# Retention of the first four chunks in whole chunks of 128 tokens, and the first pieces of the first product cut in 256 and 128 tokens

## The chip, the cores and the metric

The kernel runs on one core of a Trainium2 chip. The metric is the time of one execution on the device in microseconds; the kernel before takes 969.51 us (median of three runs, 968.78 to 971.09). The engines are named as in the profile: PE is TensorE (matrix products), PEld its loading of weights, DVE VectorE, ACT ScalarE, POOL GpSimd, SP the engine that issues most transfers.

## The reference

Retention (an attention with decay instead of a softmax) over 8 batches, 8 heads, 576 tokens and 64 columns per head, and then a feed-forward layer with a squared ReLU. All is float32.

```python
def _attn_ref(q, k, v):                      # (8, 8, 576, 64) each
    scale = 1.0 / np.sqrt(D_)
    scores = scale * np.matmul(q, k.transpose(0, 1, 3, 2))
    gamma = 1.0 - 2.0 ** (-5.0 - np.arange(H, dtype=np.float32))
    rel = pos[:, None] - pos[None, :]
    Dmat = np.where(rel >= 0, gamma[:, None, None] ** rel[None, :, :], 0.0)
    ret = scores * Dmat[None, :, :, :]
    return np.matmul(ret, v)

def _moe_ref(x, w_in, w_out):                # (4608, 512), (512, 2048), (2048, 512)
    h = np.maximum(x @ w_in, 0.0)
    return h * h @ w_out

# x: the retention's output as (batch * tokens, heads * columns)
```

## The kernel before

Each batch is cut in chunks of 128 tokens (the last has 64). A chunk is *turned* (q and k are transposed on TensorE, and the result is copied from PSUM by ScalarE and VectorE), its *scores* are computed and masked, and its output x is the sum of what its own tokens give (`own`) and what the state of all earlier tokens gives (`carry`, with the state copied to `u_sb`); the state itself grows in PSUM (`grow`). The decay stands in factors by which q and v are multiplied, so the mask holds only ones and zeros.

The kernel before works within a chunk by halves of 64 tokens. Every product then has 64 rows and 64 columns, and there is one state copy (`grown`) for each half:

```python
    def score(i, hp):
        for h in range(chunks[i][3] // CH):                     # CH = 64: two halves
            for e in range(2):
                t = slice(CH * h, CH * h + CH)
                nc.tensor.matmul(st[i]["sc"][e][rows(h), hp, :], lhsT=st[i]["kT"][rows(e), hp, t], rhs=st[i]["qT"][rows(e), hp, t],
                                 start=True, stop=True, skip_group_check=True)

    def retain_a(i):
        ...
        beside_each(own_of(i, 1, 1), grow_of(i, 0), range(0, H, 2))   # own of half 1 beside grow of half 0
        grown(i, 0)                                                    # state copy on ScalarE

    def retain_b(i):
        ...
        for h in reversed(range(cs // CH)):
            if 2 * ci + h == 0:
                continue
            u = u_sb[(2 * ci + h) % 3]
            for hp, e, b in HEADS[0:2] + HEADS[4:6] + HEADS[2:4] + HEADS[6:8]:
                s["read"] = nc.tensor.matmul(
                    x_at(hp, e, b, h), lhsT=u[rows(e), hp, :], rhs=s["qT"][rows(e), hp, CH * h:CH * h + CH], ...)

    def retain_c(i):
        ...
        own, grow = own_of(i, 0, 0), grow_of(i, 1) if more else []
        beside_each(own, grow, (0, 2))
        wait_for(st[i]["read"])
        beside_each(own, grow, (4, 6))
        x_out(i, lambda: grown(i, 1) if more else None)                # x to SBUF, then the state copy
```

The feed-forward layer works on blocks of 512 tokens. Its weights come in 64 bits and are converted on the chip, piece by piece (16 pieces of 128 columns for the first product). A piece takes six steps: three passes of VectorE and two of ScalarE, two shorter passes of VectorE ahead of them for the bits; `convert(n)` issues the next n. The first block, block 0, is multiplied piece by piece (`first_in`) while the weights are still being converted, so that TensorE has work between the chunks. A piece can run on the first 256 tokens (`halves=(0,)`) as soon as chunks 0 and 1 have given their x:

```python
    def first_in(j, halves=(0, 1)):
        ...
        for c in range(N_DM):                                          # 4
            nc.tensor.matmul(p.rearrange("p h t -> p (h t)"), lhsT=w[:, c, :], rhs=xT[0][:, c, lo * HT:hi * HT],
                             start=(c == 0), stop=(c == N_DM - 1))
        ...
        nc.scalar.activation(t, p, AF.Relu)
```

The profile shows each of these float32 products as two instructions (two MATMUL and two LDWEIGHTS).

The opening, in program order (loads and scalings left out):

```python
    scores(0); turn(1); retain_a(0); convert(3); scores(1)
    retain_b(0); retain_c(0); convert(2)
    retain_a(1); convert(4); retain_b(1); retain_c(1); convert(3)
    first_in(0, (0,)); turn(2); convert(3); first_in(1, (0,)); scores(2)
    retain_a(2); convert(2); retain_b(2); retain_c(2); convert(1)
    turn(3); convert(3); first_in(2, (0,)); scores(3); convert(3)
    retain_a(3); turn(4); convert(2); retain_b(3); retain_c(3)
    step(); step(); scores(4); convert(6); step(); convert(3); step(); convert(3)
    for i in range(N_EARLY + 1, N_CH + 1):      # the loop over the other chunks
        ...
```

`step()` runs the next part of the feed-forward layer: here the second halves of pieces 0, 1 and 2 and then piece 3 in full.

Of the kernel before, what the change touches and what calls it, by code (L numbers as in the profile page):

```python
# [9 lines left out]
F32 = mybir.dt.float32  # L10
# [30 lines left out]
def kernel(  # L41
# [91 lines left out]
    def load(i, names="qkv"):  # L133
        b, ci, c0, cs = chunks[i]
        if i == 0:
            nc.sync.dma_start(dv, decays)
        got = loaded.setdefault(i, [None] * 3)
        for name, pool, src in (("q", ld3, q), ("k", ld5, k), ("v", ld4, v)):
            if name not in names:
                continue  # L140
            t = got["qkv".index(name)] = pool.tile([128, H, D], F32, tag=name, name=f"{name}_ld")

            issue = nc.scalar if i == 0 and name != "q" else nc.sync
            at = src[b, :, c0:c0 + cs, :].rearrange("h s d -> s h d")
            if name == "v":
                issue.dma_start(t[:cs], at)
            else:

                for e in range(2):
                    issue.dma_start(t[:cs, e * HP:(e + 1) * HP, :], at[:, e::2, :])  # L150
# [6 lines left out]
    pieces += [(1, mq + mh * N_MQ, e) for mq in range(N_MQ) for mh in range(2) for e in range(2)]  # L157
    N_W1 = N_DF
    N_ALONE = 3
    N_HALF = 3  # L160
    stage = [W[5].rearrange("p (o s f) -> p o s f", o=4, s=NP),
             W[6][:, 0:3 * NP * 128].rearrange("p (o s f) -> p o s f", o=3, s=NP)]
    N_RAW = 8
# [10 lines left out]
    def rows(half, n=64):  # L174
        return slice(64 * half, 64 * half + n)
# [145 lines left out]
    def convert(count):  # L321
        for _ in range(count):
            f = next(w_in_steps, None)
            f and f()
# [18 lines left out]
    for half in range(2):  # L343
        at = slice(CH * half, CH * half + CH)
        nc.gpsimd.affine_select(
            out=msk[at, 0, 0, :], in_=msk[at, 0, 0, :], compare_op=ALU.is_ge, fill=0.0, base=0,
            pattern=[[1, CH]], channel_multiplier=-1,
        )
    u_sb = [only.tile([128, HP, D], F32, name=f"u_sb{j}") for j in range(3)]


# [9 lines left out]
    def head(hp, e):  # L361
        return 4 * (hp % 2) + 2 * e + hp // 2
# [6 lines left out]
    def clears(half, bank):  # L369

        new = (half, bank) not in clean
        clean.add((half, bank))
        return new

    def scale_q(i, engine):
        ci, cs = chunks[i][1], chunks[i][3]
        t = loaded[i][0][:cs]
        engine.tensor_tensor(t, t, dv[:cs, :, NCH + ci:NCH + ci + 1].to_broadcast([cs, H, D]), op=ALU.mult)  # L378
# [69 lines left out]
    def turn(i, engines=(0, 1)):  # L448
        turn_in(i)
        turn_out(i, engines)  # L450

    def scores(i, part=False):

        b_, ci, c0, cs = chunks[i]
        if i < N_EARLY:

            sc = [ps_f.tile([128, 512], F32, tag="f", name="sc_ps")[:, 0:256].rearrange("p (h t) -> p h t", h=HP) for e in range(2)]
        else:
            both = ps_t[0].tile([128, 2, 512], F32, tag="t", name="sc_ps")[:, :, 0:256].rearrange("p e (h t) -> p e h t", h=HP)
            sc = [both[:, e, :, :] for e in range(2)]  # L460
        st[i]["sc"] = sc
        st[i]["both"] = None if i < N_EARLY else both
        if part:
            return
        for hp in range(HP):
            score(i, hp)
        masked(i)
# [33 lines left out]
    def retain_a(i):  # L501

        b_, ci, c0, cs = chunks[i]
        xp[0] = ps_x.tile([128, 2, 256], F32, tag="x", name="x_ps", padded_shape=[128, 2, 512])
        clean.clear()
        if cs < C:
            return
        beside_each(own_of(i, 1, 1), grow_of(i, 0), range(0, H, 2))
        grown(i, 0)

    def retain_b(i):

        s = st[i]
        b_, ci, c0, cs = chunks[i]
# [6 lines that stand above are left out]
                    x_at(hp, e, b, h), lhsT=u[rows(e), hp, :], rhs=s["qT"][rows(e), hp, CH * h:CH * h + CH],  # L521
                    start=clears(b, e), stop=False, skip_group_check=True)

    def retain_c(i):

        b_, ci, c0, cs = chunks[i]
        more = ci + 1 < NCH
# [3 lines that stand above are left out]
        beside_each(own, grow, (4, 6))  # L531
        x_out(i, lambda: grown(i, 1) if more else None)

    def x_out(i, after):

        b_, ci, c0, cs = chunks[i]
        tok = b_ * S + c0
        at = tok
        p = xp[0][:, :, 0:256].rearrange("p a (g t) -> p a g t", g=2)
        while at < tok + cs:  # L540
            n = at // TOK

            while steps and steps[0][0] <= n - 2:
                if i >= N_ONE:
                    move(2)
                step()
            end = min(tok + cs, (n + 1) * TOK)
            nc.scalar.copy(xT[n][:, :, at - n * TOK:end - n * TOK].rearrange("p (g a) t -> p a g t", a=2),  # L548
                           p[:, :, :, at - tok:end - tok])
            if at == tok:  # L550
                after()
            at = end
            if n_next[0] < N_BLK and (n_next[0] + 1) * TOK <= at:
                steps.extend(block_steps(n_next[0]))
                n_next[0] += 1
        st[i] = loaded[i] = None
# [106 lines left out]
            f and f()  # L663
        del queue[:count]

    def first_in(j, halves=(0, 1)):

        assert n_made[0] > j
        wi, m, e = pieces[j]
        mp, mm = divmod(m, 2)  # L670
        p = ps_f.tile([128, 2, HT], F32, tag="f", name="h_ps")
        w = w_in[mp][:, mm, 2 * e:2 * e + 2, :, :].rearrange("p s c f -> p (s c) f")
        lo, hi = halves[0], halves[-1] + 1
        p = p[:, lo:hi, :]
        for c in range(N_DM):
            nc.tensor.matmul(p.rearrange("p h t -> p (h t)"), lhsT=w[:, c, :], rhs=xT[0][:, c, lo * HT:hi * HT],  # L676
                             start=(c == 0), stop=(c == N_DM - 1))

        t = g_room[mp % 2][:, 2:5:2, mm, :] if e else g_room[mp % 2][:, 0:4:3, mm, :]
        t = t[:, lo:hi, :]  # L680
        nc.scalar.activation(t, p, AF.Relu)

        some(2)
        queue.append(lambda: nc.vector.tensor_tensor(t, t, t, op=ALU.mult))
        if mm and e and hi == 2:
            queue.append(lambda: [nc.sync.dma_start(
                g_dram[0, a:b, :, 2 * mp:2 * mp + 2, :].rearrange("s p m t -> p s (m t)"),
                g_room[mp % 2][:, a:b, :, :].rearrange("p s m t -> p s (m t)")) for a, b in QUARTERS])
        if j >= N_W1 - 4:

            sums_w.setdefault(0, sum_w_in(0)).pop(0)()
            if n_next[0] > 1:
                if 1 not in sums_x:
                    sums_x[1] = sum_x(1)
                sums_x[1].pop(0)()
# [75 lines left out]

    def block_steps(n):
        if n == 0:
            seconds = [(0, first_in, j, (1,)) for j in range(N_HALF)]
            return seconds + [(0, first_in, j) for j in range(N_HALF, N_W1)]
        return [(n, ffn_in, n, mp, j) for mp in range(N_MP) for j in range(NP)]

    def step():
        n, f, *args = steps.pop(0)
        done[0] += 1  # L780
        f(*args)
# [77 lines left out]
    load(3)  # L859
    fetch_raw(2)  # L860
    warm(1)
    scores(0)
    turn(1)
    retain_a(0)
    convert(3)
    scores(1)
    scale_q(2, nc.gpsimd)
    retain_b(0)
    retain_c(0)
    load(4)  # L870
    fetch_raw(3)
    convert(2)
    retain_a(1)
    convert(4)
    retain_b(1)
    retain_c(1)
    load(5)
    convert(3)
    first_in(0, (0,))
    turn(2)  # L880
    convert(3)
    first_in(1, (0,))
    scores(2)
    scale_q(3, nc.gpsimd)
    retain_a(2)
    convert(2)
    retain_b(2)
    retain_c(2)
    load(6)
    convert(1)  # L890
    turn(3)
    convert(3)
    first_in(2, (0,))
    scores(3)
    scale_q(4, nc.gpsimd)
    convert(3)
    retain_a(3)
    early.close()
    ps_t[0] = first.enter_context(tc.tile_pool(name="ps_t", bufs=1, space=PS))
    turn(4)  # L900
    convert(2)
    retain_b(3)
    retain_c(3)
    load(7)
    step()
    step()
    scores(4)
    convert(6)
    scale_q(5, nc.gpsimd)
    step()  # L910
    convert(3)
    step()
    convert(3)
    for i in range(N_EARLY + 1, N_CH + 1):
# [290 lines left out]
```

## Time and profile before

| | kernel before |
|---|---|
| time, median of three runs | 969.51 us |
| span of the profiled execution | 966.2 us |
| TensorE busy | 948.0 us, 98% |
| VectorE busy | 783.2 us, 81% |
| ScalarE busy | 338.0 us, 35% |
| mean granted TensorE clock | 0.994 |

The page has the busy time of each engine, then the span in 40 equal slices of some 24 us, in which a digit is the busy share in tenths; the row PEclk is the clock that TensorE was granted, in tenths of its full speed. The other views used are the busy time by stage, and an engine's instructions in order of time. In the latter a line has the start and the length in us, the engine and the line of the code, the operation with what it writes and reads, how many there are, and in brackets how long the engine was idle before and what ended that. "issue" there means that nothing the profile shows was waited for. L432 is the turn, L473 the scores, L565 grow, L571 own, L520 carry, L676 a piece of block 0's first product, L499 the state copy, L548 the copy of x, L483 the mask and L213 to L231 the conversion of weights.

### The profile page before, as it was taken

What the parts mean: (1) busy time and instruction counts of PE and PEld (TensorE: products, weight loads), DVE (VectorE), ACT (ScalarE), POOL (GpSimd) and SP (SyncE); (2) the same over time, 40 slices, a digit from 0 to 9 for tenths busy, and PEclk for the clock granted to TensorE, in tenths of its full rate; (3) what the DMA queues carried; (4) which work ended last, traced back from release to release, by engine and by line L of the source; (5) the groups of instructions that cost most, each with busy time, mean ns of one, the idle gap of its engine ahead of it and who ended that gap; (6) DMA issues with size and microseconds to landing.
All of it is one profiled execution on the core that took longest, in us unless ns stands there. A gap on an engine that the chain in (4) does not pass through costs nothing. (4 is left out here: it accounts for less than half of the span.)

```text
span 966.2 us, 23674 instructions
## 1 busy us (share of the span) xinstructions
PE 948.0 (98%) x10002; PEld 851.0 (88%) x10002; DVE 783.2 (81%) x1447; ACT 338.0 (35%) x808; POOL 134.4 (14%) x121
## 2 busy tenths in 40 slices
PE   7899999999999999999999999999999999999998
PEld 5655688888888888878888899999999999999998
DVE  4689799988799897977966597888888787887876
ACT  3445475866765766657621000000000000000000
POOL 3301233214123123122110000000000000000000
PEclk8999999999999999999999999999999999999999
DMA  9974668677757857765178966445354454524251
GB/s 225 241 220 115 164 179 207 182 237 202 204 149 226 240 154 203 217 196 165 58 259 334 357 243 256 154 154 185 128 190 163 160 193 169 199 99 174 89 175 44
DMA packets 170730, 181.40 MB, mean 188 GB/s; under 512 B 116864, under 2 KB 131200, under 8 KB 163968
## 3 DMA queue, kind: packets, MB, share of 16 engines
q1 hardware_dynamic: 168528, 179.37, 59.7%
q8 instruction: 78, 1.28, 0.6%
q10 hardware_dynamic: 2096, 0.52, 0.2%
q14 instruction: 28, 0.23, 0.1%
HBM read 109.36 MB, written 70.52 MB: 186 GB/s over the span
## 5 line engine op out<-in xcount | busy, mean ns | idle before, releaser
L712 PE MATMUL h_b<-room,w 128*128 128x256 f32 x768 | 183.6, 382 | 2.1 <-DVE room L731 1.8
L415 ACT COPY qk<-flip 32x256 f32<-32x256 f32 x416 | 167.4, 402 | 6.1
L712 PEld LDWEIGHTS h_b<-room,w 128*128 128x128 f32 x768 | 144.1, 190 | 24.0 <-DVE room L731 3.3
L1054 PE MATMUL o_b<-w,room 128*128 128x128 f32 x1168 | 144.4, 275 | 0.2 <-DVE room L1006 0.2
L1054 PEld LDWEIGHTS o_b<-w,room 128*128 128x128 f32 x1168 | 137.3, 192 | 0.4 <-DVE room L1006 0.4
L712 PE MATMUL h_a<-room,w 128*128 128x256 f32 x512 | 122.4, 381 | 2.0 <-issue 2.0
L1054 PE MATMUL o_c<-w,room 128*128 128x128 f32 x1008 | 123.0, 275 | 0.0
L712 PE MATMUL h_c<-room,w 128*128 128x256 f32 x512 | 121.7, 380 | 0.0
L1054 PEld LDWEIGHTS o_c<-w,room 128*128 128x128 f32 x1008 | 117.7, 192 | 0.0
L712 PEld LDWEIGHTS h_a<-room,w 128*128 128x128 f32 x512 | 96.3, 190 | 15.8 <-issue 2.4
L1068 ACT COPY r<-o_a 128x128 f32<-128x128 f32 x53 | 14.1, 266 | 271.6 <-PE o_a L1054 230.9
L712 PEld LDWEIGHTS h_c<-room,w 128*128 128x128 f32 x512 | 96.7, 190 | 13.3
L1054 PE MATMUL o_a<-w,a 128*128 128x128 f32 x688 | 85.6, 275 | 0.0
L729 POOL TENSOR_TENSOR room<-room 128x512 f32<-128x512 f32 x32 | 35.9, 1121 | 336.4 <-ACT room L728 336.4
L1054 PEld LDWEIGHTS o_a<-w,a 128*128 128x128 f32 x688 | 81.2, 192 | 0.1
L719 DVE SCALAR_TENSOR_TENSOR room<-room 128x512 f32<-128x512 f32 x96 | 70.4, 733 | 3.3
L676 PE MATMUL h_ps<-room,w 128*128 128x512 f32 (+1 forms) x152 | 61.1, 551 | 2.5 <-ACT room L548 1.3
L571 PEld LDWEIGHTS x_ps<-qk,v_ld 64*64 64x64 f32 x1152 | 44.3, 135 | 19.4 <-issue 16.1
L571 PE MATMUL x_ps<-qk,v_ld 64*64 64x64 f32 x1152 | 55.4, 224 | 5.8 <-issue 2.5
L378 POOL TENSOR_TENSOR q_ld<-q_ld,dv 128x512 f32<-128x512 f32 (+1 forms) x39 | 46.4, 1189 | 87.0 <-DMA q_ld<-in_q_dram 80.7
L492 POOL TENSOR_TENSOR v_ld<-v_ld,dv 128x512 f32<-128x512 f32 (+1 forms) x40 | 53.2, 1332 | 6.6 <-DMA v_ld<-in_v_dram 6.6
L676 PEld LDWEIGHTS h_ps<-room,w 128*128 128x128 f32 x152 | 29.1, 199 | 24.4 <-issue 19.6
(105 smaller groups left out, 1348.5 us busy)
## 6 DMA issues: line engine op xcount, KB each, us to landing
g_dram<-room SPq DMA_DIRECT2D x32, 1280.0 KB, 5.7
a<-g_dram SPq DMA_DIRECT2D x30, 1024.0 KB, 6.0
room<-g_dram SPq DMA_DIRECT2D x15, 1024.0 KB, 6.1
w<-w_dram SPq DMA_DIRECT2D x7, 1792.0 KB, 11.0
out_dram<-room SPq DMA_DIRECT2D x17, 512.0 KB, 3.2
q_ld<-in_q_dram SPq DMA_DIRECT2D x64, 128.0 KB, 5.2
w<-in_moe_w_in_dram SPq DMA_DIRECT2D x16, 512.0 KB, 6.3
w<-in_moe_w_out_dram SPq DMA_DIRECT2D x16, 512.0 KB, 4.2
```

The costliest lines, as they stand in the source:

```text
L378: engine.tensor_tensor(t, t, dv[:cs, :, NCH + ci:NCH + ci + 1].to_broadcast([cs, H, D]), op=ALU.mult)
L415: nc.scalar.copy(*moves.pop(0)[2:])
L492: nc.gpsimd.tensor_tensor(vs[:cs], vs[:cs], dv[:cs, :, ci:ci + 1].to_broadcast([cs, H, D]), op=ALU.mult)
L571: return [lambda hp=hp, e=e, b=b: nc.tensor.matmul(x_at(hp, e, b, h), lhsT=s["vs"][rows(h), head(hp, e), :], rhs=s["ret"][rows(h), e, hp, ...
L676: nc.tensor.matmul(p.rearrange("p h t -> p (h t)"), lhsT=w[:, c, :], rhs=xT[0][:, c, lo * HT:hi * HT], start=(c == 0), stop=(c == N_DM - 1))
L712: nc.tensor.matmul(p[:, mm, :], lhsT=w[:, c, :], rhs=xs[n][right][:, c, :], start=(j in OPENS and mm == 0 and c == 0), stop=(j in CLOSES a ...
L719: nc.vector.scalar_tensor_tensor(t, t, 0.0, t, op0=ALU.max, op1=ALU.mult)
L729: nc.gpsimd.tensor_tensor(g["A11"], g["A11"], g["A11"], op=ALU.mult)
L1054: nc.tensor.matmul(p, lhsT=s["lefts"][left][:, m, :], rhs=w_out[j][:, m, WO_SLOT[right], :], start=(i in OPENS and m == 0), stop=(i in CLO ...
L1068: nc.scalar.copy(r[:, 0, 0:128], p)
```

## The change

In the first four chunks the products take the whole chunk of 128 tokens. The scores are 128 x 128 under a full triangular mask, own and grow contract over 128 tokens, and the state is copied once for a chunk. What this is for is half as many products and instructions and one state copy less in the chain of every chunk. The other chunks stay as they are. Of block 0, two pieces instead of three are begun early. Their first 256 tokens run after chunk 1, the tokens of chunk 2 (128) while chunk 3 is masked, and the last 128 after chunk 3. The order of turns, conversions and steps in the opening is arranged anew.

```diff
-    N_HALF = 3
+    N_HALF = 2
+    ret_room = [room[:, 7168 + j * 1024:8192 + j * 1024].rearrange("p (e a t) -> p e a t", e=2, a=HP) for j in range(2)]
+    msk_full = room[:, 9216:9344].rearrange("p (a t) -> p a t", a=1)
+    nc.gpsimd.memset(msk_full, 1.0)
+    nc.gpsimd.affine_select(... pattern=[[1, C]], channel_multiplier=-1)
...
+    def scores_full(i):
+        sc = st[i]["sc"] = [ps_f.tile([128, HP, C], F32, tag="f", name="sc_ps") for e in range(2)]
+        for hp in range(HP):
+            for e in range(2):
+                nc.tensor.matmul(sc[e][:, hp, :], lhsT=st[i]["kT"][rows(e), hp, :], rhs=st[i]["qT"][rows(e), hp, :],
+                                 start=True, stop=True, skip_group_check=True)
+        r = st[i]["ret"] = ret_room[i % 2]
+        for e in range(2):
+            nc.vector.tensor_tensor(r[:, e, :, :], sc[e], msk_full.to_broadcast([C, HP, C]), op=ALU.mult)
+        scale_v(i)
+    def carry_full(i):
+        ...
+        if chunks[i][1] == 0:
+            u_ps[0] = ps_u.tile([128, HP, D], F32, tag="u", name="u_ps")
+            return
+        u = u_sb[2 * chunks[i][1] % 3]
+        for hp, e, b in HEADS[0:2] + HEADS[4:6] + HEADS[2:4] + HEADS[6:8]:
+            nc.tensor.matmul(x_full(hp, e, b), lhsT=u[rows(e), hp, :], rhs=st[i]["qT"][rows(e), hp, :], ...)
+    def retain_full(i):
+        ci = chunks[i][1]
+        for hp, e, b in (HEADS[j] for j in (0, 4, 2, 6, 1, 5, 3, 7)):
+            nc.tensor.matmul(x_full(hp, e, b), lhsT=st[i]["vs"][:, head(hp, e), :], rhs=st[i]["ret"][:, e, hp, :], ...)
+        for hp, e, b in HEADS:
+            nc.tensor.matmul(u_ps[0][rows(e), hp, :], lhsT=loaded[i][1][:, 2 * hp + e, :], rhs=st[i]["vs"][:, head(hp, e), :], ...)
+        x_out(i, lambda: grown(i, 1))
...
-    def first_in(j, halves=(0, 1)):
+    def first_in(j, halves=(0, 1), at=(0, HT)):
...
-            seconds = [(0, first_in, j, (1,)) for j in range(N_HALF)]
+            seconds = [(0, first_in, j, (1,), (C, HT)) for j in range(N_HALF)]
...
-    scores(0)
-    turn(1)
-    retain_a(0)
+    scores_full(0)
+    turn(1, (0, 0))
+    carry_full(0)
+    retain_full(0)
     convert(3)
-    scores(1)
+    scores_full(1)
     scale_q(2, nc.gpsimd)
-    retain_b(0)
-    retain_c(0)
+    carry_full(1)
+    convert(3)
+    retain_full(1)
     load(4)
     fetch_raw(3)
-    convert(2)
-    retain_a(1)
-    convert(4)
-    retain_b(1)
-    retain_c(1)
     load(5)
     convert(3)
     first_in(0, (0,))
-    turn(2)
     convert(3)
+    turn(2, (0, 0))
+    scores_full(2)
+    scale_q(3, nc.gpsimd)
+    carry_full(2)
     first_in(1, (0,))
-    scores(2)
-    scale_q(3, nc.gpsimd)
-    retain_a(2)
-    convert(2)
-    retain_b(2)
-    retain_c(2)
+    convert(3)
+    retain_full(2)
     load(6)
-    convert(1)
     turn(3)
-    convert(3)
-    first_in(2, (0,))
-    scores(3)
+    scores_full(3)
     scale_q(4, nc.gpsimd)
     convert(3)
-    retain_a(3)
+    carry_full(3)
+    for j in range(N_HALF):
+        first_in(j, (1,), (0, C))
     early.close()
     ps_t[0] = first.enter_context(tc.tile_pool(name="ps_t", bufs=1, space=PS))
-    turn(4)
-    convert(2)
-    retain_b(3)
-    retain_c(3)
+    retain_full(3)
     load(7)
+    convert(5)
     step()
     step()
+    turn(4)
+    convert(3)
+    step()
     scores(4)
+    scale_q(5, nc.gpsimd)
     convert(6)
-    scale_q(5, nc.gpsimd)
-    step()
-    convert(3)
     step()
     convert(3)
```

In `turn(i, (0, 0))` both copies of the turned q and k are ScalarE's; otherwise ScalarE and VectorE have one each.

More of the change, by code (lines that the diff above doesn't have):

```diff
@@ L348 @@
         )
+    ret_room = [room[:, 7168 + j * 1024:8192 + j * 1024].rearrange("p (e a t) -> p e a t", e=2, a=HP) for j in range(2)]
+    msk_full = room[:, 9216:9344].rearrange("p (a t) -> p a t", a=1)
+    nc.gpsimd.memset(msk_full, 1.0)
+    nc.gpsimd.affine_select(
+        out=msk_full[:, 0, :], in_=msk_full[:, 0, :], compare_op=ALU.is_ge, fill=0.0, base=0,
+        pattern=[[1, C]], channel_multiplier=-1,
+    )
     u_sb = [only.tile([128, HP, D], F32, name=f"u_sb{j}") for j in range(3)]
@@ L532, in retain_c, with x_full @@
         x_out(i, lambda: grown(i, 1) if more else None)
+    def scores_full(i):
[8 more added lines that the diff above has]
+        scale_v(i)
+    def x_full(hp, e, b):
+        return xp[0][rows(b), e, 0:256].rearrange("p (g t) -> p g t", g=2)[:, hp % 2, :]
+    def carry_full(i):
+        xp[0] = ps_x.tile([128, 2, 256], F32, tag="x", name="x_ps", padded_shape=[128, 2, 512])
+        clean.clear()
+        if chunks[i][1] == 0:
[3 more added lines that the diff above has]
+        for hp, e, b in HEADS[0:2] + HEADS[4:6] + HEADS[2:4] + HEADS[6:8]:
+            nc.tensor.matmul(x_full(hp, e, b), lhsT=u[rows(e), hp, :], rhs=st[i]["qT"][rows(e), hp, :],
+                             start=clears(b, e), stop=False, skip_group_check=True)
+    def retain_full(i):
+        ci = chunks[i][1]
+        for hp, e, b in (HEADS[j] for j in (0, 4, 2, 6, 1, 5, 3, 7)):
+            nc.tensor.matmul(x_full(hp, e, b), lhsT=st[i]["vs"][:, head(hp, e), :], rhs=st[i]["ret"][:, e, hp, :],
+                             start=clears(b, e), stop=False, skip_group_check=True)
+        for hp, e, b in HEADS:
+            nc.tensor.matmul(u_ps[0][rows(e), hp, :], lhsT=loaded[i][1][:, 2 * hp + e, :], rhs=st[i]["vs"][:, head(hp, e), :],
+                             start=(ci == 0 and hp == 0), stop=(hp == HP - 1), skip_group_check=True)
+        x_out(i, lambda: grown(i, 1))
     def x_out(i, after):
@@ L673, in first_in @@
         lo, hi = halves[0], halves[-1] + 1
-        p = p[:, lo:hi, :]
+        p = p[:, lo:hi, at[0]:at[1]]
         for c in range(N_DM):
-            nc.tensor.matmul(p.rearrange("p h t -> p (h t)"), lhsT=w[:, c, :], rhs=xT[0][:, c, lo * HT:hi * HT],
+            nc.tensor.matmul(p, lhsT=w[:, c, :], rhs=xT[0][:, c, :].rearrange("p (h t) -> p h t", h=2)[:, lo:hi, at[0]:at[1]],
                              start=(c == 0), stop=(c == N_DM - 1))
         t = g_room[mp % 2][:, 2:5:2, mm, :] if e else g_room[mp % 2][:, 0:4:3, mm, :]
-        t = t[:, lo:hi, :]
+        t = t[:, lo:hi, at[0]:at[1]]
         nc.scalar.activation(t, p, AF.Relu)
@@ L684, in first_in @@
         queue.append(lambda: nc.vector.tensor_tensor(t, t, t, op=ALU.mult))
-        if mm and e and hi == 2:
+        if mm and e and hi == 2 and at[1] == HT:
             queue.append(lambda: [nc.sync.dma_start(
```

## The prediction

> **What bounds the kernel now.** I read the page's busy shares and slices first, then a table of busy time by stage over the first 60 us, then TensorE's own order of time, then the waits. The page:
>
> ```profile
> span 966.2 us, 23674 instructions
> ...
> PE 948.0 (98%) x10002; PEld 851.0 (88%) x10002; DVE 783.2 (81%) x1447; ACT 338.0 (35%) x808; POOL 134.4 (14%) x121
> ...
> PE   7899999999999999999999999999999999999998
> ...
> PEclk8999999999999999999999999999999999999999
> ...
> PE 40%; DVE 1%; issue 0%; DVEq 0%
> ```
>
> TensorE is busy 98% of the span, so 18.2 us in all are idle, and the chain that ended last is TensorE's. Only the first two slices (24 us each) show gaps and a lower clock, and those are where the change works. By stage (columns: window, its length, busy us and count of PE, PEld, DVE, ACT, POOL, then the granted clock, DMA share, GB/s):
>
> ```profile
> 8.00:14.50 6.50, 5.17 (x192) 4.17 (x189) 5.11 (x11) 3.59 (x7) 3.13 (x3) 1.00 1.23 279
> 14.50:20.50 6.00, 2.48 (x72) 2.10 (x69) 3.79 (x5) 2.02 (x4) 2.24 (x2) 0.63 0.97 224
> 20.50:24.40 3.90, 3.73 (x10) 2.52 (x10) 0.85 (x2) 0.39 (x2) 2.53 (x2) 0.50 0.98 254
> 24.40:32.00 7.60, 6.05 (x155) 5.06 (x156) 4.98 (x9) 2.97 (x7) 2.32 (x2) 0.87 1.17 264
> 32.00:42.00 10.00, 7.05 (x164) 5.70 (x165) 6.91 (x14) 4.51 (x10) 4.17 (x4) 1.00 0.98 212
> 42.00:50.00 8.00, 8.00 (x45) 5.67 (x44) 5.18 (x12) 3.50 (x7) 2.20 (x3) 1.00 0.96 278
> ```
>
> From 8 to 42 us TensorE idles 1.33 + 3.52 + 0.17 + 1.55 + 2.95 = 9.5 us; from 42 to 100 us it does not idle at all (58.0 busy of 58.0). A further window, 16.1 to 26.3, has clock 0.50 and 8.1 us of TensorE work: about 4 us of that are lost to the clock. So **the most that an earlier start can give is 9.5 + 4 = 13.5 us, 1.4%**. TensorE's order of time names the gaps:
>
> ```profile
> 17.05 0.26 PE L571 MATMUL x_ps<-qk,v_ld 64*64 64x64 f32 x1 [2.54 <-issue]
> ...
> 18.01 1.13 PE L520 MATMUL x_ps<-qk,u_sb 64*64 64x64 f32 x32 [0.47 <-ACT u_sb L499]
> ...
> 20.66 3.78 PE L676 MATMUL h_ps<-room,w 128*128 128x256 f32 x8 [0.67 <-ACT room L548]
> ...
> 29.48 0.27 PE L571 MATMUL x_ps<-qk,v_ld 64*64 64x64 f32 x2 [1.01 <-DVE qk L483]
> ...
> 30.71 0.69 PE L520 MATMUL x_ps<-qk,u_sb 64*64 64x64 f32 x32 [0.54 <-ACT u_sb L499]
> ...
> 35.62 0.38 PE L676 MATMUL h_ps<-room,w 128*128 128x256 f32 x1 [0.95 <-issue]
> ...
> 41.13 3.72 PE L676 MATMUL h_ps<-room,w 128*128 128x256 f32 x16 [0.59 <-ACT room L548]
> ```
>
> The largest gap, 2.54 us, waits for no engine ("issue"). Counting matmuls from the start, it falls after the 221st (442 instructions with their weight loads); the one of 0.95 us falls about 250 matmuls, so some 500 instructions, later. The DMA view by half microsecond shows one packet of the instruction queue at 14.0 to 14.5, the next at 18.5 to 19.0. I take both gaps for the arrival of instructions, with the DMA engines full (share 1.2 to 1.4 from 12 to 16). The others are the chain of one chunk: mask (1.0), state copy (0.5), x copied out (0.6).
>
> [...] Here TensorE stopped at 14.5 and the clock was 0.50 from about 16.1[...]. [...]
>
> **The change, part by part.** (1) *Work of one chunk.* Before: 32 instructions each for scores, carry and two halves of own and grow at about 15 ns, 4 x 0.5 = 2.0 us. After: 16 of each of four. A 128-column instruction alone takes 124 ns (144.4 us over 1168, group L1054, o_b), so with two tiles 62, with four 31; grow streams 64 columns with two tiles, 37. Scores 16 x 62 = 1.0, carry 16 x 31 = 0.5, own 1.0, grow 0.6: 3.1 us. **TensorE gets no less work, but about 1 us more per chunk**, half of it beside the mask it would wait for. (2) *Instructions.* 64 matmuls instead of 128 in a chunk, each with a weight load: 500 fewer in all. A block of 256 took 3.6 us before the 2.54 us gap. It will now take some 9, where fetching needed about 6 (11 to 17.05), so both issue gaps, 3.5 us, go. (3) *Waits.* One state copy per chunk instead of two, and it lies behind the next chunk's scores: the 0.5 us gaps go. (4) *Masks.* 512 columns from PSUM instead of 256: 2 x 0.6 instead of 2 x 0.34 us on VectorE, +0.5 per chunk, partly on the path; both turn copies of chunks 1 and 2 on ScalarE, one after the other, +0.5 each. (5) *Pieces.* Two are split 256 + 128 + 128 instead of three by 256 + 256: 8 x 124 ns = 1.0 per quarter, 8 x 239 = 1.9 per half, equal within 0.1 us. The quarters fill the mask wait of chunk 3.
>
> The new order in time, from the same durations: scores 0 at 8.8, turn 1 until 10.4, mask 0 until 11.25, retain 0 until 12.35; scores 1 until 13.35, mask 1 until 14.75, retain 1 until 15.85 (before 20.0). Piece 0 is converted behind mask 1, so at 17.3, and its half runs until 19.2; turn 2, two copies and scores 2 until 22.1, carry, half of piece 1 until 24.5, retain 2 until 26.1; turn 3 and copies 27.7, scores 3 until 28.7, carry and two quarters until 31.2, retain 3 until 32.8, x out at 33.5. Data is there: in GpSimd's order of time the scaling of v, which waits for the load, begins at 11.8 for chunk 1, 18.3 for chunk 2 and 23.0 for chunk 3. Before, this point is 41.13: **7.6 us earlier**. At that point 2 quarters, piece 2 in full and turn 4 are owed (2.0 + 3.63 + 0.65 = 6.3) against 3 halves (5.7): minus 0.6. The conversion of weights is half a piece behind by program order (35 conversion steps written ahead of the loop against 38, six to a piece); VectorE has 9.6 us free from 42 to 100, but a stall or two, about 0.5 us, may show. Net **about 7 us: 969.5 - 7 = 962.5**.
>
> **The rivals.** *The clock falls anyway.* From 15.85 to 17.3 TensorE waits for piece 0 and works thinly around it. If the clock halves for 10 us again, 3 to 4 us of the gain go: about 966. I give it three in ten. *128x64 does not run in pairs.* Then own and grow cost 16 x (124 + 70) = 3.1 instead of 1.6: 1.5 more per chunk, 6 in all, about 968. For it speaks that no such shape is in the trace; against it, own and grow with 64 rows already put two column halves side by side at 15 ns. *Weights become the bound.* VectorE is 85 to 90% busy from 60 to 100; if pieces come late, TensorE gets gaps there and the gain melts, 965 to 969. Against it: it idled 35% until 42 and is fed in the same order. *All goes better*: shapes pair at 55 ns and the chain closes up, 9 us, 960.
>
> **Range and chances.** The ceiling of 13.5 us is 1.4%, so faster by over 2% is next to excluded; slower by over 2%, 19 us, would need a new wait in the dense part. 962.5, range 958 to 967.
>
> **What would show it.** Right: no issue gap over 0.5 us before 42; clock 1.00 from 14 to 30; scores at about 62 ns per instruction; the first 16 matmuls of the second halves near 33.5; TensorE without gaps from then on. Wrong: clock 0.50 after 16 us; own at 124 ns apart; gaps in front of the pieces (L676) waiting for VectorE or ScalarE between 35 and 100; x of chunk 3 later than 36.

## The result, and the profile after

The changed kernel takes **964.78 us** (four runs, 964.09 to 964.94) against 969.14 us of the kernel before in the same comparison: ratio 0.9954, 95% interval 0.9932 to 0.9976. It is faster by 4.4 us; 7 were predicted. The changed kernel scatters by 0.9 us. The kernel before scatters far more: its runs in all comparisons lie mostly between 964 and 971 us, and its median in a comparison between 967.1 and 969.1 us. Against the largest of these comparisons (28 runs, 967.47 us) the changed kernel would be only 2.7 us faster.

The same rows of the page as before the change:

```profile
span 963.2 us, 23158 instructions
...
PE 947.4 (98%) x9754; PEld 849.4 (88%) x9754; DVE 784.6 (81%) x1446; ACT 337.4 (35%) x807; POOL 134.5 (14%) x123
...
PEclk9999999999999999999999999999999999999999
```

In the changed kernel L439 is the turn, L450 its copy, L547 the scores, L551 the mask, L573 own, L576 grow, L722 a piece of block 0's first product, L594 the copy of x and L758 the first product of block 1. TensorE has 248 products fewer, no slice with a lower clock any more, and, over the whole span, the same busy time. By stage (columns as in the prediction):

```profile
8.00:14.50 6.50, 5.81 (x103) 4.92 (x106) 3.77 (x6) 3.43 (x7) 3.38 (x3) 1.00 1.22 277
14.50:20.50 6.00, 4.41 (x68) 3.51 (x60) 5.66 (x9) 2.91 (x6) 2.12 (x2) 1.00 1.01 224
20.50:24.40 3.90, 2.74 (x42) 2.23 (x38) 2.55 (x5) 1.07 (x2) 2.47 (x2) 1.00 0.96 258
24.40:32.00 7.60, 6.70 (x102) 5.82 (x100) 3.89 (x7) 3.06 (x7) 2.11 (x2) 1.00 1.18 266
32.00:42.00 10.00, 9.52 (x85) 6.40 (x84) 8.53 (x17) 4.84 (x11) 3.45 (x3) 1.00 1.08 227
42.00:50.00 8.00, 7.34 (x43) 3.15 (x45) 7.79 (x13) 3.62 (x8) 2.85 (x2) 1.00 1.07 310
...
60.00:80.00 20.00, 18.46 (x248) 9.28 (x240) 17.42 (x28) 8.26 (x17) 5.86 (x5) 1.00 0.61 161
80.00:100.00 20.00, 18.17 (x210) 9.06 (x211) 17.28 (x29) 9.18 (x17) 3.08 (x3) 1.00 0.33 93
```

Read the clock first: 1.00 in every row, where 0.50 to 0.87 stood. Then TensorE's busy time: from 60 to 100 us, where it had no gap before, 3.4 us are idle now. TensorE's list of waits (line waited for: us in total, times, longest) and its order of time say for what:

```profile
PE h_ps L722 <- DVE w L231: 5.6, 6, 1.4
```

```profile
18.04 1.97 PE L722 MATMUL h_ps<-room,w 128*128 128x256 f32 x8 [1.32 <-DVE w L231]
...
33.97 2.05 PE L722 MATMUL h_ps<-room,w 128*128 128x128 f32 x16 [0.22 <-ACT room L594]
...
41.17 3.70 PE L722 MATMUL h_ps<-room,w 128*128 128x512 f32 x8 [0.26 <-DVE w L231]
46.18 3.70 PE L722 MATMUL h_ps<-room,w 128*128 128x512 f32 x8 [0.66 <-DVE w L231]
...
66.06 3.70 PE L722 MATMUL h_ps<-room,w 128*128 128x512 f32 x8 [1.38 <-DVE w L231]
...
80.79 3.70 PE L722 MATMUL h_ps<-room,w 128*128 128x512 f32 x8 [0.94 <-DVE w L231]
...
95.61 3.70 PE L722 MATMUL h_ps<-room,w 128*128 128x512 f32 x8 [1.04 <-DVE w L231]
```

The point that the prediction followed, the first products behind the x of chunk 3, comes at 33.97 instead of 41.13 us, 7.2 us earlier. The wait of 1.32 us in front of piece 0 lies ahead of this point, so it is in the 7.2 us already. The other five, 4.3 us of idle time, lie behind it: pieces of weights wait for the last pass of their conversion (L231), and the head start is spent. The first product of block 1, in the kernel before and in the changed one:

```profile
106.74 1.99 PE L712 MATMUL h_a<-room,w 128*128 128x256 f32 x8
```

```profile
105.68 1.99 PE L758 MATMUL h_a<-room,w 128*128 128x256 f32 x8
```

Only **1.1 us are left** at this point. Yet the spans of these two profiles differ by 3.0 us (966.2 and 963.2). The other 2.0 us come where neither the change nor the prediction looked. The kernel before has this line, and the changed kernel has no gap there:

```profile
419.82 1.35 PE L712 MATMUL h_a<-room,w 128*128 128x256 f32 x5 [1.99 <-issue]
```

Three questions follow. Is the lost head start a matter of order, or is VectorE full? Is it the whole-chunk products that made the start earlier? And what is the gap at 420 us?

### The profile page after: what moved, and what is told of

Same layout as the page of the kernel before. It is cut to its first block, busy times and chain, and to the rows that moved or that the text cites. A ratio compares the mean times of both kernels' runs of the same rounds, so it can differ in the third digit from the quotient of the medians.

```text
span 963.2 us, 23158 instructions
## 1 busy us (share of the span) xinstructions
PE 947.4 (98%) x9754; PEld 849.4 (88%) x9754; DVE 784.6 (81%) x1446; ACT 337.4 (35%) x807; POOL 134.5 (14%) x123
## 5 line engine op out<-in xcount | busy, mean ns | idle before, releaser
L758 PE MATMUL h_b<-room,w 128*128 128x256 f32 x768 | 183.7, 382 | 2.3 <-DVE room L777 1.8
L758 PEld LDWEIGHTS h_b<-room,w 128*128 128x128 f32 x768 | 144.1, 190 | 24.0 <-DVE room L777 3.3
L758 PE MATMUL h_a<-room,w 128*128 128x256 f32 x512 | 122.1, 381 | 0.0
L758 PE MATMUL h_c<-room,w 128*128 128x256 f32 x512 | 121.7, 380 | 0.0
L758 PEld LDWEIGHTS h_a<-room,w 128*128 128x128 f32 x512 | 96.4, 190 | 13.8 <-issue 0.4
L758 PEld LDWEIGHTS h_c<-room,w 128*128 128x128 f32 x512 | 96.7, 190 | 13.3
L722 PE MATMUL h_ps<-room,w 128*128 128x512 f32 (+2 forms) x160 | 59.9, 519 | 5.8 <-DVE w L231 5.6
L722 PEld LDWEIGHTS h_ps<-room,w 128*128 128x128 f32 x160 | 26.7, 190 | 30.2 <-issue 20.4
L617 PEld LDWEIGHTS x_ps<-qk,v_ld 64*64 64x64 f32 x1024 | 38.8, 134 | 13.0 <-issue 12.3
L777 DVE TENSOR_TENSOR room<-h_b,room 128x512 f32<-128x512 f32 x32 | 21.9, 685 | 33.5 <-PE h_b L758 33.5
```

The costliest lines, as they stand in the source:

```text
L617: return [lambda hp=hp, e=e, b=b: nc.tensor.matmul(x_at(hp, e, b, h), lhsT=s["vs"][rows(h), head(hp, e), :], rhs=s["ret"][rows(h), e, hp, ...
L722: nc.tensor.matmul(p, lhsT=w[:, c, :], rhs=xT[0][:, c, :].rearrange("p (h t) -> p h t", h=2)[:, lo:hi, at[0]:at[1]], start=(c == 0), stop= ...
L758: nc.tensor.matmul(p[:, mm, :], lhsT=w[:, c, :], rhs=xs[n][right][:, c, :], start=(j in OPENS and mm == 0 and c == 0), stop=(j in CLOSES a ...
L777: nc.vector.tensor_tensor(g["A22"], p, p15, op=ALU.add)
```

## The experiments

All numbers are medians. The ratios are to the kernel before, with their 95% intervals.

### More converted weights in hand

```diff
     first_in(0, (0,)); convert(3); turn(2, (0, 0))
+    convert(3)
     scores_full(2); scale_q(3, nc.gpsimd); carry_full(2); first_in(1, (0,)); convert(3); retain_full(2)
     load(6); turn(3)
+    convert(3)
     scores_full(3); scale_q(4, nc.gpsimd)
-    convert(3)
+    convert(5)
     ...
     retain_full(3); load(7)
-    convert(5)
+    convert(3)
```

> The changed kernel with the conversion of weights moved ahead in program order, by half a piece before the scores of chunk 2 and by more before and after the scores of chunk 3, so that 41 conversion steps stand ahead of the loop instead of 35. Theory (the gain that is missing was lost to weights that come late because they stand late in the order; VectorE and ScalarE were idle from 21 to 31 us): the waits of the pieces for VectorE (5.6 us in the changed kernel) fall under 1.5 us, the first product of block 1 starts near 101 to 102 us instead of 105.7, and the time falls to about 960 to 961 us. Rival (VectorE has no capacity left between 32 and 60 us, whatever the order): the waits stay at 4 us or more and the time stays at 964 to 965 us.

Measured: **959.43 us**, ratio 0.9909 (0.9887 to 0.9932), 5.35 us less than the changed kernel. Its waits of pieces for VectorE:

```profile
PE h_ps L722 <- DVE w L231: 1.8, 1, 1.8
```

This one wait is that of piece 0 at 17.8 us; the later ones are gone. (So the 1.5 us expected for all waits were missed by this one, and the time came out lower than expected.) The first products behind the x of chunk 3, and the first of block 1:

```profile
33.75 2.05 PE L722 MATMUL h_ps<-room,w 128*128 128x128 f32 x16 [0.22 <-ACT room L594]
...
100.23 1.99 PE L758 MATMUL h_a<-room,w 128*128 128x256 f32 x8
```

Block 1 comes 5.45 us earlier than in the changed kernel, which is the whole gain. Between the two lines lie 66.48 us, in the changed kernel 71.71 for the same work. So its five late waits cost **5.2 us**, some 0.2 us each more than the idle time that is marked. From 21 to 31 us the busy time of VectorE rises from 4.97 to 8.99 us of 10:

```profile
21.00:31.00 10.00, 8.29 (x127) 7.05 (x128) 4.97 (x10) 3.54 (x8) 4.13 (x4) 1.00 1.13 261
```

```profile
21.00:31.00 10.00, 8.52 (x129) 7.27 (x130) 8.99 (x15) 4.84 (x10) 3.53 (x4) 1.00 1.12 253
```

The first row is the changed kernel's, the second this one's. VectorE was not full; its idle half lay ahead of the conversions that were late. What it waited for there shows in the changed kernel's order of time of VectorE:

```profile
22.99 1.29 DVE L551 TENSOR_TENSOR room<-sc_ps,room 128x512 f32<-128x512 f32 x2 [1.32 <-PE sc_ps L547]
...
27.69 0.69 DVE L450 COPY qk<-t_ps 128x512 f32<-128x512 f32 x1 [2.40 <-PE t_ps L439]
...
29.69 1.29 DVE L551 TENSOR_TENSOR room<-sc_ps,room 128x512 f32<-128x512 f32 x2 [1.31 <-PE sc_ps L547]
```

These three waits, two masks and one copy of a turn that wait for TensorE, are all of its 5.0 us of idle time. The rival falls.

### Whole chunks in the old order, and the new order with halves

The first undoes the order and the cut of the pieces, the second undoes the whole chunks.

```diff
 # whole chunks, old order: N_HALF = 3, halves of 256, and in the opening of the kernel before
-    scores(i) ... retain_a(i) ... retain_b(i); retain_c(i)
+    scores_full(i) ... carry_full(i) ... retain_full(i)
 # new order, halves: in the opening of the changed kernel
-    scores_full(i) ... carry_full(i) ... retain_full(i)
+    scores(i) ... retain_a(i) ... retain_b(i); retain_c(i)
```

> Whole-chunk products in the order and with the three half pieces of the kernel before (38 conversion steps ahead of the loop). Theory: no issue gap before 40 us, clock 1.00 throughout, x of chunk 3 out at about 36 us, and fewer waits for weights than in the changed kernel (under 3 us), so a time of 963 to 966 us. Rival (the new order is what makes whole chunks worth it): x of chunk 3 at 39 us or later and 967 to 969 us.

> The new order of the opening and the new cut of the pieces, but the first four chunks by halves of 64 tokens as in the kernel before. Theory (the whole-chunk products carry the earlier start): the issue gap of 2 to 3 us near 14 to 17 us is back, x of chunk 3 is out at 37 us or later, and as the order has the smaller lead of converted weights, the time is 967 to 970 us, no better than the kernel before. Rival (the order alone brings the gain): x of chunk 3 near 34 to 35 us and a time of 964 to 966 us.

Measured: whole chunks in the old order **962.65 us**, 0.9946 (0.9929 to 0.9964); the new order with halves **971.79 us**, 1.0037 (1.0024 to 1.0049), slower than the kernel before. In the first no issue gap stands before 40 us, the clock is 1.00 and the x of chunk 3 begins to be copied at 34.12 (after the change: 33.34; in the kernel before: 40.49). In the second the x comes at 40.93, with issue gaps of 1.42 us at 16.8 and 0.65 at 40.6, and clock 0.57 from 20.5 to 24.4. Of the two parts of the change, the whole chunks bring the earlier start (in the old order 1 to 2 us earlier than expected), and the new order gives part of it away: block 1 begins at 101.25 in the old order, against 105.68. The second run shows no more than that the new order does not help halves as it stands; it was not tried with the issue gaps moved, which the section on blocks does for the kernel before.

### Twice the instructions for the same products

```diff
-                nc.tensor.matmul(sc[e][:, hp, :], lhsT=..., rhs=st[i]["qT"][rows(e), hp, :], ...)
+                for t in (slice(0, CH), slice(CH, C)):
+                    nc.tensor.matmul(sc[e][:, hp, t], lhsT=..., rhs=st[i]["qT"][rows(e), hp, t], ...)
 # carry and own likewise; grow by 32 columns twice
```

> The changed kernel with each whole-chunk product of the first four chunks cut in two along the streamed columns: twice the instructions again, as in the kernel before, with the same masks, state copies and order. Theory (the number of TensorE instructions counts by itself, as they come in blocks that arrive late): gaps marked issue of 1 to 3 us return between 13 and 20 us, the clock may fall to 0.5 behind them, x of chunk 3 is out 2 to 5 us later than 34, though part of it is hidden behind the wait for weights; time 965.5 to 968 us. Rival (only the state copies and the chain of waits count): no such gap, x of chunk 3 within 1 us of 34, time within 0.7 us of the changed kernel.

Measured: **972.88 us**, 1.0044 (1.0028 to 1.0061), worse than either expectation. The x of chunk 3 is copied from 40.29, 7 us later than in the changed kernel, yet the only issue gap of the opening is one of 0.22 us at 18.2. The experiment did not test what it was meant to. The groups between 8 and 46 us, of the split kernel and of the changed one:

```profile
L548 PE MATMUL sc_ps<-qk 64*128 64x64 f32 x128 | 8.4, 280 | 2.3 <-DVE qk L450 1.2 <-ACT qk L450 1.2
L576 PE MATMUL x_ps<-room,v_ld 128*64 128x64 f32 x128 | 5.1, 227 | 0.7 <-DVE room L552 0.4 <-issue 0.2
L580 PE MATMUL u_ps<-v_ld,k_ld 128*64 128x32 f32 x128 | 4.6, 221 | 0.0
```

```profile
L547 PE MATMUL sc_ps<-qk 64*128 64x128 f32 x64 | 4.6, 284 | 2.3 <-DVE qk L450 1.2 <-ACT qk L450 1.2
L573 PE MATMUL x_ps<-room,v_ld 128*64 128x128 f32 x64 | 4.5, 281 | 0.7 <-DVE room L551 0.7
L576 PE MATMUL u_ps<-v_ld,k_ld 128*64 128x64 f32 x64 | 2.5, 222 | 0.0
```

Half as many streamed columns in each, and yet nearly the same time for each instruction: scores 66 ns against 72, grow 36 against 39 (busy over count). The own products (x_ps) do gain, 40 ns against 70. Scores and grow now stream half as many columns as their weights have, own as many as its weights have. So I read it that in scores and grow the load of the weights sets the pace, and it was doubled too. The order of time of the loads agrees: in the split kernel the 32 loads for the scores of chunk 0 take 1.91 us, 60 ns each, and the 32 for its grow 1.07 us, 33 ns each, hardly less than the products, and the 128 weight columns of the scores cost about twice the 64 of grow. As the products took longer, the instructions were used up more slowly too (the 128 products ahead of the gap in 4.94 us, against 3.42 in the kernel before), which is how I explain that only 0.22 us of gap are left. In this profile the clock falls as well: 0.83 in the row from 32 to 42 us, which is 3.4 us at 0.50, and the carry products at 35.15 take 1.20 us instead of 0.76. Since 24.7 us the longest stop of TensorE ahead of them is 0.91 us.

### Where a block of instructions ends

To move block ends without touching the work, idle products are added to or taken from the warm-up, in which TensorE has no loaded data anyway (in the kernel before its first product on such data starts at 5.68 us). In the kernel before, 128 instructions more (64 products and 64 loads), then 256:

```diff
-    warm(5)
+    warm(1)
+    t = ps_f.tile([128, 512], F32, tag="f", name="idle_ps")
+    for _ in range(36):          # second run: 68, of 16 columns
+        nc.tensor.matmul(t[0:32, 0:32], lhsT=idle[:, 0:32], rhs=idle[:, 0:1].to_broadcast([128, 32]), start=True, stop=True)
```

> The kernel before with 64 more TensorE instructions and their weight loads in the warm-up ahead of chunk 0 (36 small products on idle data in place of 4 wide ones): 128 instructions, so that all later ones stand half a block of 256 further on. Theory (the gap of 2.5 us at 14.4 us is the arrival of a block): the gap moves about 64 TensorE products earlier in the program, to the products of chunk 0's own half or carry near 12 us, or falls under 1 us, and is not at the own products of chunk 1 near 14 to 17 us. Rival (it waits for a transfer or an engine that the profile does not name): the gap stays in front of the own products of chunk 1 near 14 to 17 us.

> The kernel before with 68 small products on idle data in place of 4 wide ones in the warm-up: 256 TensorE instructions more, so that block ends fall at the same places of the program as in the kernel before. The warm-up may last 1 to 3 us longer. Theory (the place of a block's end makes the gap): the gap of 1 to 2.5 us is back in front of the own products of chunk 1, some 5 to 6 us after the scores of chunk 0 began, so is the one near 420 us, and the time is 966 to 971 us. Rival (the small products of the warm-up, by their kind, removed the gap in the run with 36 of them): no gap over 1 us there, 962 to 965 us.

Measured: with 128 more **962.29 us**, 0.9964 (0.9946 to 0.9983), though all of its work is that of the kernel before and its first scores start 0.8 us later. Four of its six runs, with a mean clock of 1.00, take 961.9 to 962.3 us, less than any run of the changed kernel; in the other two (965.4 and 966.4 us) the clock is lower again, 0.996 and 0.993. With 256 more 971.28 us, 1.0038 (1.0025 to 1.0051). The first issue gap of each, 128 first:

```profile
17.93 0.21 PE L571 MATMUL x_ps<-qk,v_ld 64*64 64x64 f32 x1 [0.85 <-issue]
```

```profile
22.06 0.21 PE L571 MATMUL x_ps<-qk,v_ld 64*64 64x64 f32 x1 [1.98 <-issue]
```

With 256 more, a whole block, the gap stands where it did: six products before the end of the first own and grow group of chunk 1, as in the kernel before (the warm-up is 3.9 us longer and the first scores start 5.6 us later, so the time can't be compared). The gap near 420 us is back too (2.11 us at 422.28), the small one near 35 us is not. With half a block the first gap has left that place. What remains is 0.85 us behind the 284th product of the old program, just where the next block end is expected: 220, 128 products on and 64 back. The clock stays at 1.00 in this profile, from 14.5 to 20.5 us it had been 0.63:

```profile
14.50:20.50 6.00, 4.07 (x104) 3.44 (x104) 5.71 (x7) 2.70 (x6) 2.88 (x2) 1.00 0.96 229
```

The expectation near 12 us was wrong; there the block came in time. Of the alternative stated with it, the size holds, under 1 us; the gap is still at own products of chunk 1, but at the last of them, 64 products on.

The trace also shows the arrival itself. The view of the DMA queues from 14.0 to 14.5 us of the kernel before has this line; 16.4% of 16 engines' half microsecond are the 1.31 us that the one packet took:

```profile
q8 instruction: 1, 0.02, 16.4%
```

The packet, of 16 KB, runs from 14.28 to 15.59 us, and TensorE goes on at 17.05. That is 1.46 us after the packet. The other issue gaps over 0.2 us of the two kernels end in the same way after such a packet: in the kernel before 1.48 us (at 35.62) and 1.55 us (at 419.82), in the changed kernel 1.51 us (its only one, 0.24 us long, at 356.60). The packets also give the size of a block. In the kernel before the queue has 78 of them, of 16 KB each. Between its first gap and its second stand 512 TensorE instructions (products, loads of weights and those of the sequencer) and two packets, between the first and the one at 420 us 9985 and 39: 256 a packet. Counted from the first product, the first gap of the versions that have one in the opening always stands behind 220 products (the prediction counted 221) or, in both padded kernels, 348, which is 128 more. And its length goes with the use of instructions: the 128 products ahead of this place took 3.42 us in the kernel before (gap 2.54 us), 4.05 with half a block more (0.85), 4.94 in the split kernel (0.22) and 11.0 in the changed kernel, which has no gap.

The kernel before once more, for a second profile:

> The kernel before once more, unchanged, for a second profile. Theory (blocks end at fixed places of the program): gaps marked issue at the same three places, own of chunk 1 near 14 to 17 us, the first half of piece 2 near 35 us and L712 near 420 us, of like length. Rival (chance): gaps elsewhere or none; time 964 to 971 us either way.

Measured: 966.22 us in one execution. The gaps stand at the same three products, at 15.77 (1.35 us), 33.98 (1.22) and 418.05 (2.20). The first is 1.2 us shorter than in the first profile and ends 1.3 us earlier, and block 1 begins 1.9 us earlier (104.83). So the length of this gap varies from run to run, and so does the stretch of low clock: 6.8 us at 0.50 here, 10.24 in the first profile. In the opening of the other profiles in which the clock falls there, the rows by stage add up to 3.4 us at 0.50 (the split kernel), 6.8 (256 more) and 10.2 (the new order with halves). This explains at least part of the scatter of the kernel before.

Now the gap near 420 us. The kernel before has 10002 products, whole chunks in the old order 9746: exactly 256, or 512 instructions, fewer. The latter has the gap too, while the changed kernel (9754), the version with more weights in hand (9754) and the new order with halves (10010), all 16 instructions further on, have none there. Two runs move it on purpose: eight products fewer in the warm-up of the version with more weights in hand, and eight more in that of whole chunks in the old order.

```diff
 # more weights in hand, shifted
-    warm(5)  ...  warm(3)
+    warm(2, 512); warm(1)  ...  warm(1, 512)        # products of 512 columns instead of 256
 # whole chunks in the old order, shifted
     warm(5)
+    for _ in range(4):
+        nc.tensor.matmul(t[0:32, 0:16], lhsT=idle[:, 0:32], rhs=idle[:, 0:1].to_broadcast([128, 16]), start=True, stop=True)
```

> The version with more converted weights in hand, and eight TensorE instructions with their eight weight loads fewer in the warm-up ahead of the first chunk (fewer, wider products on idle data): the same work, but all that follows stands 16 instructions earlier, where it stood in the kernel before modulo 256. Theory (instructions come in blocks of 256, and the gap of 2.0 us near 420 us of the kernel before comes from where a block ends; whole chunks in the old order, exactly 512 instructions shorter, have it too): a gap marked issue of about 2 us comes back near 410 to 415 us in front of a product of L758, and the time is 961 to 962 us instead of 959.4. Rival (that gap is chance or a matter of transfers at that time): no gap there, time 959 to 960 us.

> Whole-chunk products in the old order, with four small idle products (eight instructions and their weight loads) more in the warm-up, so that what follows stands as in the changed kernel modulo 256. Theory (the gap of 2.1 us near 414 us of whole chunks in the old order is the end of a block): no gap over 0.5 us there, time 960.3 to 961.2 us instead of 962.65. Rival: the gap stays, time 962 to 963.5 us.

Measured: **960.84 us** against 959.43 in the first, 0.9938 (0.9924 to 0.9952), with the gap; **959.80 us** against 962.65 in the second, 0.9924 (0.9896 to 0.9951), and the gap is gone. The gap in whole chunks in the old order before the shift, and in the shifted first:

```profile
414.07 1.56 PE L758 MATMUL h_a<-room,w 128*128 128x256 f32 x6 [2.06 <-issue]
```

```profile
412.84 1.02 PE L758 MATMUL h_a<-room,w 128*128 128x256 f32 x4 [1.79 <-issue]
```

It depends on where the program stands modulo 256 instructions: in the kernel before it stands behind product 5189, with a block more behind 5317, in these two behind 4932 and 4934. Without this gap, whole chunks in the old order take 959.42 to 960.53 us, the changed kernel 964.09 to 964.94. So the new order, with its cut of the pieces, was a loss. The changed kernel escaped it because two pieces cut in three have eight products more than three pieces cut in two.

### The two turns moved ahead

```diff
 # in the version with more weights in hand
+    turn(2, (0, 0))
     load(5); convert(3); first_in(0, (0,)); convert(3)
-    turn(2, (0, 0)); convert(3)
+    convert(2)
     scores_full(2)
+    convert(1)
     scale_q(3, nc.gpsimd); carry_full(2)
+    turn(3)
     first_in(1, (0,)); convert(3); retain_full(2); load(6)
-    turn(3)
     convert(3); scores_full(3)
```

> The version with more converted weights in hand, and in it the turn of chunk 2 ahead of the half of piece 0 and the turn of chunk 3 ahead of the half of piece 1, so that their copies run beside a piece instead of in front of the scores. Theory (what is left in the opening are these waits: 1.8 us in front of piece 0, 1.2 and 0.9 us in front of the scores): two of the three waits go, x of chunk 3 is out near 31 to 32 us, the first product of block 1 begins near 98 to 99 us, time 957 to 958.5 us. Rival (weights become the bound again): waits of pieces for VectorE of 2 us or more between 30 and 60 us, time 959 to 960 us.

Measured: **957.62 us**, 0.9907 (0.9891 to 0.9923), the fastest of all; the x of chunk 3 is copied from 31.11 and block 1 begins at 98.23. All three waits are gone, one more than expected (the 0.3 us left in front of scores are those of chunk 0, as in the changed kernel); a wait of 1.0 us for the transfer of k of chunk 2 is new. No piece waits for VectorE any more. It beats both kernels: by 7.2 us the changed one, which is the difference of medians from two comparisons.

## Why the prediction was right in its range and high in its gain

**What bounds the kernel.** Right. The ceiling of 13.5 us for the opening was not passed by any version (the best, 957.62 us, is 9.5 us under the kernel before in its own comparison, 967.08, and some 2 us of that are the gap at 420). That gap was not in the ceiling, since the prediction counted only the first 42 us.

**Work of one chunk.** Right in size and in sign. In the changed kernel's order of time 16 score instructions take 0.97 us, carry 0.60, own 1.00, grow 0.56: 3.1 us, as worked out. The pairs of 128x64 run side by side (16 own instructions in 1.00 us are 63 ns each, against 124 for one of 128 columns alone), and that rival is out. How many products of a shape run at once was the prediction's estimate; the kernel before shows two rates for it, 32 score instructions that start in 0.5 us (15 ns each) and 8 transposes of 64x128 in 0.30 us (37 ns each).

**Instructions.** Right: no gap marked issue before 42 us, and the clock stays at 1.00. The block of 128 products took 11.0 us where some 9 were predicted; its arrival had been reckoned at 6. But the credit is narrower than the prediction gave. Half a block of idle instructions does nearly the same for the old products. Block 1 begins at 100.90 there and at 100.63 in the shifted whole chunks in the old order, although the padded kernel starts its first scores 0.3 us later than that one. So in the opening these two versions come out alike, and what the whole chunks bring is above all a use of instructions slow enough for the next block to arrive (128 products in 11.0 us against 3.42). The block of 256 instructions that the prediction reckoned with is what the counts between packets show. How far ahead of its use a block can arrive was not measured; the 6 us for its arrival were an estimate.

**The new order in time.** Right: x out at 33.5 predicted, copied from 33.3 us on (by the first products behind it: 33.97). The mask (1.29 us), the two copies of a turn on ScalarE (1.07) and the two quarters (2.05) took what was reckoned.

**Lead of the converted weights.** This is the step that failed: "a stall or two, about 0.5 us, may show". Five waits behind that point cost 5.2 us, and the sign named for a wrong prediction, pieces that wait for VectorE between 35 and 100 us, came true. The mechanism was named, half a piece less in hand, but it was sized by VectorE's free time from 42 to 100 us as a whole. What counts is where the free time lies. By program order the conversion stood behind masks and copies that wait for TensorE, and in these traces VectorE stood idle in front of them (5.0 us from 21 to 31 us) and did not take the conversion first. The rival of late weights had been given 965 to 969 us, and the argument against it, "fed in the same order", was the mistake.

**Sum.** The prediction's own terms, 7.6 less 0.6 less 0.5, give 6.5, which it rounded up to 7. Measured are 7.2 us earlier, less 0.9 owed (6.3 us of work against 5.4; the prediction had 6.3 against 5.7), less 5.2 for the five waits: 1.1, as at block 1. The gap at 420 us, 2.0, stood in no part of the prediction and makes 3.0 in the profiles. The medians give 4.4; the rest is the scatter of the kernel before, whose profiled run lay below its median (968.0 against 969.1). That 964.8 us lies well inside the range is partly luck: with a gap of 2.0 us like that of the kernel before it would have been 966.8, just below the upper end of 967.

## What to carry to other kernels

When an opening is made shorter for one engine, check the order of each engine that feeds it, and not its free time in sum: half a piece of lead cost 5.2 us here of the 7.2 that had been won. A gap of TensorE marked issue in a stretch of many small products may be the end of an instruction block; look for a packet of the instruction queue that ends some 1.5 us before the gap does (1.46 to 1.55 in the traces of the two kernels, at DMA shares of 1.17, 0.69 and 1.20 in the three gaps of the kernel before). A few idle instructions ahead of it are a cheap test, and took 3.5 us (by the ratio) to 4.8 us (by the medians) off the time here. And before a gain is put down to a change, look for gaps that merely moved, even 400 us behind it.

## What was not expected of the hardware

A product of 64 streamed columns with 128 weight columns is hardly faster than one of 128 (66 against 72 ns in a stream of them). Eight products more or less in the warm-up take away or bring back a stop of about 2 us near 415 us (medians apart by 2.9 and 1.4 us). The third is how little it takes to lose the clock: where an issue gap of 1.3 to 2.5 us stands between 14 and 22 us, 7 to 10 us at half clock begin during it or up to 2 us after its end. Which stop suffices is not shown: the changed kernel has waits of 1.2 to 1.3 us at 18 and 21.8 us and keeps its clock, and the split kernel lost it near 35 us with no stop over 0.91 us since 24.7.
